# First batch of a conv and MLP-mixer kernel: convolution halo in four row quarters, and another order of its loads, decodes and stores

## The chip, the core and the metric

The kernel runs on one core of a Trainium2 chip. Its engines are TensorE (PE, with a weight load PEld beside the matmuls), VectorE (DVE), ScalarE (ACT), GpSimd (POOL) and SyncE (SP), each with a queue of its own that runs in order, and 16 DMA engines. The metric is the device time of one launch in microseconds, lower is better.

## The reference

```python
# x (8, 4096, 192) float32, weight (8, 7); w_tok1 (4096, 256), w_tok2 (256, 4096),
# w_ch1 (192, 1536), w_ch2 (1536, 192) are float64
w = softmax(weight, axis=-1)                     # 8 heads of 24 channels, 7 taps
x_pad = concat([zeros(B, 6, D), x], axis=1)
xc[b, s, h, g] = sum_k w[h, k] * x_pad[b, s + k, h, g]          # causal convolution
h = maximum(xc.T @ w_tok1, 0) @ w_tok2           # token mixing, for each channel
u = xc + h.T
out = u + maximum(u @ w_ch1, 0) @ w_ch2          # channel mixing, for each token
```

## The kernel before

The eight batches go in groups: the first batch alone, then pairs. The 4096 tokens of a batch are 32 blocks of 128; block `j` holds tokens `128 j` to `128 j + 127` on the partitions. Large products run on TensorE as three products of a high and a low part (`hi*hi + hi*lo + lo*hi`). The four weights come from HBM in 64-bit form, are loaded as pairs of 32-bit words (`dec_raw`, `early_raw`) and put together on chip: one ACT step (Abs, L196) and four VectorE steps (L198, L199, L202, L205), and, where high and low parts are needed, a cast on ACT (L211) and a difference on VectorE (L212). They are all decoded once, during the first batch. Four buffers hold raw words; a load into one waits until the decode before it in that buffer has ended.

`stage1_first` runs the first batch up to token mixing:

- The convolution runs on TensorE. `make_band` builds, from the softmax of the taps `cw`, a `band` matrix per head (128x128, the taps within a block) and a `corner` matrix per head (the 6 tokens that come from the block before). It multiplies and reduces on VectorE (L493, L497), moves the pieces to their place with small matmuls (`moved`, L488) and copies them out on ACT (L504, L507). `keep_busy(n)` issues n transposes of the identity whose results nobody reads.
- The blocks go in four chunks of eight. `x0_load(c)` loads a chunk; chunks 1 to 3 bring the last block of the chunk before once more (9 blocks). `conv_mm(m)` does four heads of a chunk: for each a band matmul on its blocks (L522) and a corner matmul on the blocks one earlier (L523), both over 128 rows. `conv_out(m)` copies the sums to `xc_0`, `xc_1`, `xc_2` and, for the fourth chunk, `u` (L532).
- Eight jobs decode w_tok1, four blocks each, to `t_0` to `t_7`; one decodes half of w_tok2 to `t2s`; three decode thirds of w_ch1 to `w_hi`, `w_lo`. `work` and `behind` say between which decodes the matmuls of convolution and token mixing (`mix`, L453) and the copies stand. `begin(n)` issues a job's ACT step, `woven` its VectorE steps, interleaved with another job's, `next_load()` the next load on SP. After the last job come three loads for w_ch2 (`w2f`) and one for the other half of w_tok2.
- `xc_store(c)` writes the convolved chunks to HBM (`xcd`, on SP), `t1_store(i)` the decoded w_tok1 (`t1d`, on POOL); both are read again by later groups.

The hooks after it are the first batch's second half: `first_mix` (`mix2`: the product with `t2s`, added to `u`), `first_transposed` (the identity matmuls and casts to `own_hi`, `own_lo`), and `first_channel1` for six pairs `p` (L1080, relu to `h_first` on ACT, L1092). `load_u` and `load_next` copy the first four convolved blocks on POOL (L1058) for the first and the second group of tokens. `after()` gives up the pool `p0`, in whose place later tiles such as `h_first` are laid; an instruction that writes there first waits for all users of what lay there.

In later groups the convolution runs on ACT and VectorE (L658, L660) from loads `raw` (L648). A planner, `bg`, sets their place among the matmuls from estimated costs; `bg.lands(9e3)` tells it that a load takes 9 us.

Everything is put on the queues in the order of this code; no scheduler moves instructions.

Of the kernel before, what the change touches and what calls it, by code (L numbers as in the profile page):

```python
# [8 lines left out]
F32 = mybir.dt.float32  # L9
# [130 lines left out]
def conv_mixer_kernel(ctx: ExitStack, tc: tile.TileContext, x, weight, w_tok1, w_tok2, w_ch1, w_ch2, out):  # L140
    nc = tc.nc
    B, S, D = x.shape
    H, K = weight.shape
    G = D // H
# [246 lines left out]

    def stage1_first(pe, p0, pd, late, load_u, load_next, after, thirds, hooks):
        b = GROUPS[0][0]
# [3 lines left out]
        dec = Decoder(pd, 1024, 4, 3)  # L397
        BC = P // 4
        BR = BC + HALO
# [26 lines left out]
        homes = [(pe if c else p0).tile([P, NC + 1, D], F32, name=f"x0_{c}") for c in range(len(chunks))]  # L426
        xcs += [p0.tile([P, NC, D], F32, name=f"xc0_{c}") for c in range(len(chunks) - 1)]
        tops = [p0.tile([P, TJ * JT], F32, name=f"t1_{i}") for i in range(NJ // TJ)]

        def x0_load(c):  # L430
            x0 = homes[c]
            x0s.append(x0)
            j0 = chunks[c].start
            if c == 0:
                nc.gpsimd.memset(x0[:, 0, :], 0.0)
                nc.sync.dma_start(out=x0[:, 1:], in_=xt[:, 0:NC])
            else:
                nc.sync.dma_start(out=x0, in_=xt[:, j0 - 1:j0 + NC])

# [43 lines left out]
        def make_band():  # L483
# [16 lines left out]
            for hs in halves:  # L500
                ps = ps_x.tile([P, P // BC, H2, BC], F32, name="ps_x")
                for b0 in range(P // BC):
                    moved(ps[:, b0], b0 * BC - HALO, hs)
                nc.scalar.copy(out=band[:, hs].rearrange("p h (b c) -> p b h c", c=BC), in_=ps)  # L504
                ps = ps_x.tile([P, H2, BC], F32, name="ps_x")
                moved(ps, P - HALO, hs)
                nc.scalar.copy(out=corner[:, hs, 0:BC], in_=ps)  # L507
                if hs.start == 0:
                    keep_busy(9)

        def conv_mm(m):
            c, part = m // 2, m % 2
            x0 = x0s[c]
            n = NC
            for h2 in range(part * H // 4, (part + 1) * H // 4):
                ps = ps_x.tile([P, TT], F32, name="ps_x")
                convs.setdefault(m, []).append((h2, ps))
                for i in range(2):
                    h = 2 * h2 + i
                    o = ps[:, i * n * G:(i + 1) * n * G].rearrange("p (j g) -> p j g", g=G)  # L520
                    hs = slice(h * G, (h + 1) * G)
                    nc.tensor.matmul(out=o, lhsT=band[:, h], rhs=x0[:, 1:, hs], start=True, stop=False)  # L522
                    nc.tensor.matmul(out=o, lhsT=corner[:, h], rhs=x0[:, :n, hs], start=False, stop=True)  # L523

# [36 lines left out]
        next_load()  # L561
        begin(0)
        make_band()
# [8 lines left out]
        for n in range(nj - 1):  # L572
            if n + 2 < nj:
                begin(n + 1)
            if n == 1:
                conv_mm(2)
            for m in behind.get(n, ()):
                conv_out(m)
            chains = [chains_a[n - 1][2:] if n else [], chains_a[n][:2]]

            if n in (len(quads) - 1, len(quads)):
                woven(chains.pop(0))
            woven(*chains, split(n - 2) if n > 1 and "top" not in jobs[n - 2] else [])
            if n + 2 == nj:
                begin(n + 1)
            for fn in work.get(n, ()):
                fn()
            if n not in (0, 6, 9):
# [6 lines left out]
            if n == 7:  # L595
                load_u(xcs[0])
            if n == 9:
                late()
        n = nj - 1
        mix1_done(0, accs)  # L600
        woven(split(n - 2))
        hooks[0]()
        hooks[1]()
        woven(chains_a[n - 1][2:], chains_a[n][:2])
        next_load()
        woven(split(n - 1))
        load_next(xcs[0])
        for i in range(len(quads)):
            t1_store(i)
        after()  # L610
        hooks[2]()
        woven(chains_a[n][2:])
        next_load()
        woven(split(n))
        for jb, st in zip(later, sts[nj:]):
# [9 lines left out]
    def stage1(gi, pools):  # L625
# [276 lines left out]

    def mix2(gi, q, t2, u, at_once=False, turned=None):
        nb = len(GROUPS[gi])
# [8 lines left out]
        for j in range(TJ):  # L913
# [152 lines left out]

    def first_mix():
        mix2(0, 0, *first["u"], at_once=True)

# [115 lines left out]
    def first_done():  # L1185
# [218 lines left out]
```

## Time and profile before

| | |
|---|---|
| median of 3 runs | 2025.3 us (2024.91 to 2025.76) |
| profiled execution | 2024.59 us |
| its span on the core | 2022.8 us |
| mean granted TensorE clock | 0.998 |
| busy: PE, PEld, DVE, ACT, POOL | 2006.7, 1862.9, 1505.6, 777.0, 218.5 us |
| bytes moved | 260.93 MB, 129 GB/s over the span |

The span is the time from the first to the last record on the core; the execution's own time is 1.8 us more. Busy shares are averages over the whole span, while the change lies in its first 120 us; so the windows and the timelines of that stretch are what to read. In a timeline a row gives start and duration in us, engine, line, operation, and what ended the idle time before it. "SPq" is an issue of a DMA on SP, and its duration holds the time in which SP waited to issue it.

### The profile page before, as it was taken

Reading aid. Unit: us, or ns where it says so; the run is one execution under the profiler, and the core shown is the slowest. Engines: PE = TensorE matmul, PEld = TensorE weight load, DVE = VectorE, ACT = ScalarE, POOL = GpSimd, SP = SyncE. Lnnn points to the kernel's source line nnn. Section 1 sums busy time; section 2 is a strip of 40 time slices with the busy share of each in tenths; the row PEclk is TensorE's granted clock in tenths of the full one; section 3 lists DMA queues with packets and bytes.
Section 4 is the critical chain, followed back from the end, with each engine's and each line's share of the span. In section 5 each row is a group of like instructions: output and inputs, shape, how many; then the busy total and the mean of one; then the engine's idle time right before and its main releaser. Section 6 shows DMA issues by size and latency. Waiting matters only on the chain.

```text
span 2022.8 us, 44729 instructions
## 1 busy us (share of the span) xinstructions
PE 2006.7 (99%) x18667; PEld 1862.9 (92%) x18667; DVE 1505.6 (74%) x3008; ACT 777.0 (38%) x1280; POOL 218.5 (11%) x380
## 2 busy tenths in 40 slices
PE   9999999999999999999999999999999999999999
PEld 9889999999999999998999999999999999999998
DVE  7799998998759998856975689556666666666664
ACT  4676554544333434323333334232233222333322
POOL 0100000001211011110111100111111010011110
PEclk9999999999999999999999999999999999999999
DMA  9855446455455567424664335433233232333310
GB/s 308 282 160 169 132 156 207 155 163 186 132 154 143 155 189 203 125 67 123 170 162 116 106 93 150 146 95 80 53 77 79 74 84 67 79 84 85 85 48 17
DMA packets 280089, 260.93 MB, mean 129 GB/s; under 512 B 188624, under 2 KB 227280, under 8 KB 279888
## 3 DMA queue, kind: packets, MB, share of 16 engines
q1 hardware_dynamic: 257360, 179.80, 31.5%
q0 software_dynamic: 22528, 78.27, 12.9%
q8 instruction: 148, 2.42, 0.5%
q14 instruction: 53, 0.43, 0.1%
HBM read 146.60 MB, written 71.30 MB: 108 GB/s over the span
## 4 chain that ended last, share of the span: by engine, by line
PE 91%; DVE 4%; DMA 2%; SPq 1%; ACT 1%; issue 0%; POOL 0%; ACTq 0%; DVEq 0%
PE ps_x L1080 36%; PE ps_x L1139 23%; PE ps_x L1156 12%; PE ps_x L1157 5%; PE ps_x L959 2%; DVE xc L660 2%; PE ps_a L767 2%; PE ps_a L768 2%; PE ps_a L769 2%; DMA dec_raw<-in_moe_w_tok_dram 1%; DVE hl L1122 1%; PE ps_a L453 1%; PE ps_x L927 1%; PE ps_x L924 1%; PE ps_x L929 1%; PE ps_x L928 1%
## 5 line engine op out<-in xcount | busy, mean ns | idle before, releaser
L1121 ACT ACTIVATE hh<-ps_x 128x512 fp32r<-128x512 f32 x756 | 410.9, 596 | 838.3 <-PE ps_x L1080 838.1
L1122 DVE SCALAR_TENSOR_TENSOR hl<-ps_x,hh 128x512 fp32r<-128x512 f32 x756 | 484.6, 685 | 190.9 <-ACT hh L1121 189.7
L1139 PE MATMUL ps_x<-w,hh 64*128 64x384 f32 x3360 | 483.2, 356 | 2.7 <-ACT hh L1121 2.7
L1139 PE MATMUL ps_x<-w,hl 64*128 64x192 f32 x3360 | 422.0, 248 | 0.4 <-DVE hl L1122 0.4
L660 DVE SCALAR_TENSOR_TENSOR xc<-raw,cw,xc 128x384 f32<-128x384 f32 (+1 forms) x768 | 388.1, 560 | 11.1 <-ACT xc L658 11.1
L1156 PE MATMUL ps_x<-w,hh 128*128 128x384 f32 x1344 | 387.6, 360 | 0.0
L1157 PE MATMUL ps_x<-w,hl 128*128 128x192 f32 x1344 | 336.5, 250 | 0.0
L1080 PE MATMUL ps_x<-other,w_hi 64*128 64x512 f32 x1296 | 336.3, 388 | 0.0
L1080 PE MATMUL ps_x<-own_hi,w_hi 64*128 64x512 f32 x1440 | 331.9, 392 | 1.6 <-ACT own_hi L989 0.6
L1080 PE MATMUL ps_x<-own_lo,w_hi 64*128 64x512 f32 x1440 | 325.9, 388 | 0.0
L1080 PE MATMUL ps_x<-own_hi,w_lo 64*128 64x512 f32 x1440 | 325.8, 388 | 0.0
L1139 PEld LDWEIGHTS ps_x<-w,hl 64*128 64x128 f32 x3360 | 322.2, 188 | 1.8 <-DVE hl L1122 0.9
L1139 PEld LDWEIGHTS ps_x<-w,hh 64*128 64x128 f32 x3360 | 316.2, 185 | 3.9 <-ACT hh L1121 2.9
L1157 PEld LDWEIGHTS ps_x<-w,hl 128*128 128x128 f32 x1344 | 256.6, 191 | 0.0
L1080 PEld LDWEIGHTS ps_x<-other,w_hi 64*128 64x128 f32 x1296 | 235.9, 184 | 22.3
L1156 PEld LDWEIGHTS ps_x<-w,hh 128*128 128x128 f32 x1344 | 252.4, 188 | 0.4 <-DVE hl L1122 0.4
L1080 PEld LDWEIGHTS ps_x<-own_hi,w_hi 64*128 64x128 f32 x1440 | 212.9, 185 | 31.0 <-issue 4.4
L1080 PEld LDWEIGHTS ps_x<-own_hi,w_lo 64*128 64x128 f32 x1440 | 217.8, 185 | 25.1
L1080 PEld LDWEIGHTS ps_x<-own_lo,w_hi 64*128 64x128 f32 x1440 | 218.0, 185 | 24.8
L1080 PE MATMUL ps_x<-other,w_lo 64*128 64x512 f32 x648 | 181.4, 386 | 0.0
L1147 DVE TENSOR_TENSOR osb<-ps_x,osb 128x192 f32<-128x192 f32 x420 | 150.2, 358 | 25.4 <-PE ps_x L959 0.5
L1145 DVE TENSOR_TENSOR osb<-ps_x,u 128x192 f32<-128x192 f32 x140 | 49.8, 356 | 134.9 <-PE ps_x L1139 134.9
(164 smaller groups left out, 2423.6 us busy)
## 6 DMA issues: line engine op xcount, KB each, us to landing
raw<-in_x_dram SPq DMA_DIRECT2D x56, 672.0 KB, 7.2
t<-t2d SPq DMA_DIRECT2D x64, 512.0 KB, 5.7
u<-xcd SPq DMA_DIRECT2D x62, 384.0 KB, 7.3
xcd<-xc POOLq DMA_DIRECT2D x28, 768.0 KB, 8.0
t<-t1p SPq DMA_DIRECT2D x32, 512.0 KB, 4.4
out_dram<-osb POOLq DMA_DIRECT2D x36, 384.0 KB, 3.5
out_dram<-osb SPq DMA_DIRECT2D x27, 384.0 KB, 3.1
t2d<-stage SPq DMA_DIRECT2D x16, 512.0 KB, 4.8
```

What stands on the lines that cost most here:

```text
L660: nc.vector.scalar_tensor_tensor(out=dst, in0=src, scalar=cw[:, h, k:k + 1], in1=dst, op0=ALU.mult, op1=ALU.add)
L767: nc.tensor.matmul(out=ps, lhsT=wh, rhs=xh, start=a, stop=False)
L768: nc.tensor.matmul(out=ps, lhsT=wh, rhs=xl, start=False, stop=False)
L769: nc.tensor.matmul(out=ps, lhsT=wl, rhs=xh, start=False, stop=z)
L1080: nc.tensor.matmul(out=ps, lhsT=w1[w][rows, t[h][2][c], p * P:(p + 1) * P], rhs=t[h][v][rows, c], start=n == 0, stop=n == len(prods) - 1,)
L1121: nc.scalar.activation(out=h["hh", f], in_=ps, func=AF.Relu)
L1122: nc.vector.scalar_tensor_tensor(out=h["hl", f], in0=ps, scalar=0.0, in1=f32(h["hh", f]), op0=ALU.max, op1=ALU.subtract)
L1139: nc.tensor.matmul(out=ps[:, :m], lhsT=h[part, f][ks, ts], rhs=w2[ks, f, :m], start=n == 0 and part == "hh", stop=z and part == "hl",)
L1145: nc.vector.tensor_tensor(out=rows(osb[:, j]), in0=rows(pss[0][:, :D]), in1=tokens(u, i)[:, j], op=ALU.add)
L1147: nc.vector.tensor_tensor(out=osb[:, j], in0=v, in1=osb[:, j], op=ALU.add)
L1156: nc.tensor.matmul(out=ps[:, :2 * D], lhsT=h["hh", f][:, ts], rhs=w2[:, f, :], start=n == 0, stop=False)
L1157: nc.tensor.matmul(out=ps[:, :D], lhsT=h["hl", f][:, ts], rhs=w2[:, f, :D], start=False, stop=z)
```

## The change

1. Halo: `corner` becomes `[P, 4, 2, P]`. Each pair of heads uses 6 rows at partition 0, 32, 64 or 96, so that the corner matmuls take 6 rows and lie in four row quarters, one after the other in the queue. Their other operand is a new tile `halo`, filled by four loads of 6 partitions x 31 blocks x 48 channels on ACT's queue. The chunks are then loaded with 8 blocks each.
2. Band: pieces of 16 columns instead of 32 (`BC = P // 8`), so that VectorE's operations become 22x448 instead of 38x896 and there are twice the small matmuls; `keep_busy` 34 and 4 instead of 54 and 9; the first job's ACT step stands behind the first band copies.
3. Loads: the first weight load is ahead of the first x load. The job of w_tok2 comes ahead of the last of w_tok1.
4. Stores: `xc_store` stood ahead of the second w_ch2 load; now chunks 3 and 0 follow the third w_ch2 load, chunks 1 and 2 the w_tok2 load after it. `t1_store` stays behind `load_next`.
5. `mix2` takes VectorE steps of the first w_ch1 third between its adds; the two other thirds begin later.
6. `t_0` to `t_7`, `xc_1`, `xc_2` lie in a new pool `p1`, given up after `stage1_first`; `xc_0` stays in `p0`.
7. `bg.lands` is told 12 us instead of 9 for the first load of each group of pairs.

```diff
-        BC = P // 4
+        BC = P // 8
...
-        corner = p0.tile([P, H, P], F32, name="corner")
+        corner = p0.tile([P, NQ, 2, P], F32, name="corner")
         nc.gpsimd.memset(corner, 0.0)
+        halo = p0.tile([P, NJ, 2 * G], F32, name="halo")
+        nc.gpsimd.memset(halo[:, 0], 0.0)
+        for g in range(NQ):
+            nc.scalar.dma_start(
+                out=halo[g * QB:g * QB + HALO, 1:], in_=xt[P - HALO:, :NJ - 1, 2 * g * G:2 * (g + 1) * G]
+            )
...
-                nc.sync.dma_start(out=x0, in_=xt[:, j0 - 1:j0 + NC])
+            nc.sync.dma_start(out=x0, in_=xt[:, chunks[c].start:chunks[c].stop])
...
-        jobs = [t1_job(i) for i in range(len(quads))] + [t2_job(0, 0, TT)] + [w1_job(ps) for ps in thirds]
+        nt = len(quads) - 1
+        jobs = [t1_job(i) for i in range(nt)] + [t2_job(0, 0, TT), t1_job(nt)] + [w1_job(ps) for ps in thirds]
...
-                moved(ps, P - HALO, hs)
-                nc.scalar.copy(out=corner[:, hs, 0:BC], in_=ps)
+                for n, g in enumerate(gs):
+                    moved(ps[:, n], g * QB, slice(2 * g, 2 * (g + 1)))
+                nc.scalar.copy(out=corner[:, gs.start:gs.stop, :, 0:BC], in_=ps)
                 if hs.start == 0:
-                    keep_busy(9)
+                    begin(0)
+                    keep_busy(4)
...
-                    nc.tensor.matmul(out=o, lhsT=band[:, h], rhs=x0[:, 1:, hs], start=True, stop=False)
-                    nc.tensor.matmul(out=o, lhsT=corner[:, h], rhs=x0[:, :n, hs], start=False, stop=True)
+                    nc.tensor.matmul(out=sums(ps, i), lhsT=band[:, h], rhs=x0[:, :, hs], start=i == 0, stop=False)
+            if part:
+                for i in range(2):
+                    for g, ps in convs[m - 1] + convs[m]:
+                        rs = slice(g * QB, g * QB + HALO)
+                        nc.tensor.matmul(
+                            out=sums(ps, i), lhsT=corner[rs, g, i],
+                            rhs=halo[rs, chunks[c].start:chunks[c].stop, i * G:(i + 1) * G], start=False, stop=i == 1,
+                        )
...
+        next_load()
         x0_load(0)
-        next_load()
-
-        keep_busy(54)
+        keep_busy(34)
...
-            6: [lambda: mix(4), lambda: mix(5)], 8: [lambda: mix(6, 7)],
+            6: [lambda: mix(4), lambda: mix(5)], 7: [lambda: mix(6)],
...
-            if n == 8:
-                for c in (3, 0, 1, 2):
-                    xc_store(c)
...
+        load_u(xcs[0])
+        woven(chains_a[nt][2:])
+        woven(split(nt))
+        woven(chains_a[nt + 1])
+        mix(nt)
...
         mix1_done(0, accs)
-        woven(split(n - 2))
-        hooks[0]()
+        hooks[0](chains_a[nt + 2][2:])
...
-        woven(split(n - 1))
+        woven(split(nt + 3))
+        for c in (3, 0):
+            xc_store(c)
         load_next(xcs[0])
-        for i in range(len(quads)):
-            t1_store(i)
         after()
         hooks[2]()
-        woven(chains_a[n][2:])
+        woven(chains_a[nt + 4][2:])
         next_load()
-        woven(split(n))
+        woven(split(nt + 4))
+        for c in (1, 2):
+            xc_store(c)
+        for i in range(len(quads)):
+            t1_store(i)
...
-                    done["load", q2, part] = bg.lands(9e3)
+                    done["load", q2, part] = bg.lands(9e3 if q2 else 12e3)
```

VectorE's queue at the end of the w_tok1 decodes, before. `t_7` is the last block of w_tok1; the first `dec_top` of 128x1024 is the half of w_tok2, those of 128x768 are thirds of w_ch1:

```order
L205 SCALAR_TENSOR_TENSOR t_6_131<-dec_raw,t_6_131 128x1024
L198 TENSOR_SCALAR t_7_132<-t_7_132 128x1024
L199 TENSOR_SCALAR t_7_132<-t_7_132 128x1024
L202 SCALAR_TENSOR_TENSOR t_7_132<-dec_raw,t_7_132 128x1024
L205 SCALAR_TENSOR_TENSOR t_7_132<-dec_raw,t_7_132 128x1024
L198 TENSOR_SCALAR dec_top<-dec_top 128x1024
L199 TENSOR_SCALAR dec_top<-dec_top 128x1024
L202 SCALAR_TENSOR_TENSOR dec_top<-early_raw,dec_top 128x1024
L198 TENSOR_SCALAR dec_top<-dec_top 128x768
L205 SCALAR_TENSOR_TENSOR dec_top<-early_raw,dec_top 128x1024
```

The same place after the change:

```order
L205 SCALAR_TENSOR_TENSOR t_6_140<-dec_raw,t_6_140 128x1024
L198 TENSOR_SCALAR dec_top<-dec_top 128x1024
L199 TENSOR_SCALAR dec_top<-dec_top 128x1024
L202 SCALAR_TENSOR_TENSOR dec_top<-dec_raw,dec_top 128x1024
L205 SCALAR_TENSOR_TENSOR dec_top<-dec_raw,dec_top 128x1024
L212 TENSOR_TENSOR t2s<-dec_top,t2s 128x2x512
L198 TENSOR_SCALAR t_7_141<-t_7_141 128x1024
L199 TENSOR_SCALAR t_7_141<-t_7_141 128x1024
L202 SCALAR_TENSOR_TENSOR t_7_141<-early_raw,t_7_141 128x1024
L205 SCALAR_TENSOR_TENSOR t_7_141<-early_raw,t_7_141 128x1024
```

The five steps of the w_tok2 half, its low part (L212) with them, moved ahead of the last block of w_tok1.

SP's queue around the stores of the convolution, before. `x2` stands for two in a row; `in_moe_w_ch_dram` of 128x4x384 is w_ch2, `in_moe_w_tok_dram` of 128x2x1024 the other half of w_tok2, `raw` the next batches' x:

```order
L538 DMA xcd_75<-xc_1_123 128x1536
L538 DMA xcd_75<-xc_2_124 128x1536
L232 DMA dec_raw<-in_moe_w_ch_dram 128x4x384 x2
L232 DMA dec_raw<-in_moe_w_tok_dram 128x2x1024
L648 DMA raw_759<-in_x_dram 128x14x96
```

After:

```order
L553 DMA xcd_75<-xc_0_131 128x1536
L232 DMA dec_raw<-in_moe_w_tok_dram 128x2x1024
L553 DMA xcd_75<-xc_1_132 128x1536
L553 DMA xcd_75<-xc_2_133 128x1536
L670 DMA raw_753<-in_x_dram 128x14x96
```

The stores moved behind the w_ch2 loads (two of them ahead of, two behind the w_tok2 load); ahead of the first row shown stands now `xcd<-u` and ahead of that the last w_ch2 load.

ACT's queue at the first channel mixing, after, where the waits of an instruction stand in brackets (DMAHW4 is the landing of a load or store that SP issued, here of `xcd<-xc_0`; Pool is the second copy of `xc_0`):

```order
L211 CAST w_hi<-dec_top 128x3x256 [waits DVE_49]
L1116 ACTIVATE h_first<-ps_x 128x512 [waits DMAHW4_49,PE_49,Pool_49]
L1116 ACTIVATE h_first<-ps_x 128x512 [waits PE_49]
L211 CAST w_hi<-dec_top 128x3x256 [waits DVE_49]
L196 ACTIVATE w2f<-dec_raw 128x768 [waits DMAHW0_49]
```

Before the change these rows are the same but for line and semaphore numbers; what moved is the place of the store and of the copy that the second row waits for.

More of the change, by code (lines that the diff above doesn't have):

```diff
@@ L388, in mix1_accs, with stage1_first @@
         return [ps_a.tile([P, TT], F32, name=f"ps_a{kc}") for kc in range(KC)]
-    def stage1_first(pe, p0, pd, late, load_u, load_next, after, thirds, hooks):
+    def stage1_first(pe, p0, p1, pd, late, load_u, load_next, after, thirds, hooks):
         b = GROUPS[0][0]
@@ L422, in stage1_first @@
         band = p0.tile([P, H, P], F32, name="band")
[L423 removed]
+        corner = p0.tile([P, NQ, 2, P], F32, name="corner")
         nc.gpsimd.memset(corner, 0.0)
[L426 to L428 removed]
+        halo = p0.tile([P, NJ, 2 * G], F32, name="halo")
[4 more added lines that the diff above has]
+            )
+        homes = [(pe if c else p0).tile([P, NC, D], F32, name=f"x0_{c}") for c in range(len(chunks))]
+        xcs += [(p1 if c else p0).tile([P, NC, D], F32, name=f"xc0_{c}") for c in range(len(chunks) - 1)]
+        tops = [p1.tile([P, TJ * JT], F32, name=f"t1_{i}") for i in range(NJ // TJ)]
         def x0_load(c):
@@ L504, in make_band @@
                 nc.scalar.copy(out=band[:, hs].rearrange("p h (b c) -> p b h c", c=BC), in_=ps)
-                ps = ps_x.tile([P, H2, BC], F32, name="ps_x")
-                moved(ps, P - HALO, hs)
-                nc.scalar.copy(out=corner[:, hs, 0:BC], in_=ps)
+                ps = ps_x.tile([P, 2, 2, BC], F32, name="ps_x")
+                gs = range(hs.start // 2, hs.stop // 2)
+                for n, g in enumerate(gs):
+                    moved(ps[:, n], g * QB, slice(2 * g, 2 * (g + 1)))
+                nc.scalar.copy(out=corner[:, gs.start:gs.stop, :, 0:BC], in_=ps)
                 if hs.start == 0:
-                    keep_busy(9)
+                    begin(0)
+                    keep_busy(4)
         def conv_mm(m):
@@ L514, in conv_mm, with sums @@
             n = NC
+            def sums(ps, i):
+                return ps[:, i * n * G:(i + 1) * n * G].rearrange("p (j g) -> p j g", g=G)
             for h2 in range(part * H // 4, (part + 1) * H // 4):
@@ L561, in stage1_first @@
         next_load()
-        begin(0)
         make_band()
@@ L569, in stage1_first @@
             4: [lambda: mix(2), lambda: mix(3)], 5: [lambda: conv_mm(6), lambda: conv_mm(7)],
-            6: [lambda: mix(4), lambda: mix(5)], 8: [lambda: mix(6, 7)],
+            6: [lambda: mix(4), lambda: mix(5)], 7: [lambda: mix(6)],
         }
-        for n in range(nj - 1):
-            if n + 2 < nj:
+        for n in range(nt + 1):
+            if n < nt:
                 begin(n + 1)
@@ L578, in stage1_first @@
                 conv_out(m)
+            if n == nt:
+                begin(n + 1)
             chains = [chains_a[n - 1][2:] if n else [], chains_a[n][:2]]
-            if n in (len(quads) - 1, len(quads)):
+            if n == nt:
                 woven(chains.pop(0))
-            woven(*chains, split(n - 2) if n > 1 and "top" not in jobs[n - 2] else [])
-            if n + 2 == nj:
-                begin(n + 1)
+            woven(*chains)
             for fn in work.get(n, ()):
                 fn()
-            if n not in (0, 6, 9):
+            if n not in (0, 6):
                 next_load()
@@ L901, in conv_mixer_kernel, with mix2 @@
     NQ = P // QB
-    def mix2(gi, q, t2, u, at_once=False, turned=None):
+    def mix2(gi, q, t2, u, at_once=False, turned=None, between=()):
         nb = len(GROUPS[gi])
@@ L932, in mix2 @@
                 two, one = flat(u)[:, j, 0], flat(u)[:, j, 1]
+                if between:
+                    between.pop(0)()
                 if not at_once:
@@ L1065, in first_next, with first_mix @@
         first["next"] = first_load(xc, TJ)
-    def first_mix():
-        mix2(0, 0, *first["u"], at_once=True)
+    def first_mix(between):
+        mix2(0, 0, *first["u"], at_once=True, between=between)
     def first_transposed():
@@ L1172, in conv_mixer_kernel @@
     hp = None
-    pe_ctx, p0_ctx, pd_ctx, ht_ctx = (ExitStack() for _ in range(4))
+    pe_ctx, p0_ctx, p1_ctx, pd_ctx, ht_ctx = (ExitStack() for _ in range(5))
     pe = pe_ctx.enter_context(tc.tile_pool(name="pe", bufs=1))
     pd = pd_ctx.enter_context(tc.tile_pool(name="pd", bufs=1, side="right"))
+    p1 = p1_ctx.enter_context(tc.tile_pool(name="p1", bufs=1, side="right"))
     p0 = p0_ctx.enter_context(tc.tile_pool(name="p0", bufs=1, side="right"))
```

31 lines of the change are left out of this document (15 added, 16 removed).

## The prediction

> **What bounds the kernel now.** I read the page's busy times and chain first, then its first 140 us by windows, then the timelines of the engines there.
>
> ```profile
> PE 2006.7 (99%) x18667; PEld 1862.9 (92%) x18667; DVE 1505.6 (74%) x3008; ACT 777.0 (38%) x1280; POOL 218.5 (11%) x380
> PE 91%; DVE 4%; DMA 2%; SPq 1%; ACT 1%; issue 0%; POOL 0%; ACTq 0%; DVEq 0%
> ```
>
> PE is busy 2006.7 of 2022.8 us, and 91% of the chain is PE's. What the first batch loses at its end stays lost: nothing behind it has slack worth a microsecond. Everything that the change touches, but for one number in the planner, lies in the first 120 us. By windows (span; then busy us and instructions of PE, PEld, DVE, ACT, POOL; PE clock, DMA share, GB/s):
>
> ```profile
> 25.00:30.40 5.40, 5.40 (x33) 5.40 (x34) 5.13 (x7) 2.06 (x4) 0.77 (x1) 1.00 1.05 383
> 61.10:66.40 5.30, 4.51 (x20) 2.96 (x21) 4.46 (x7) 4.63 (x7) 5.04 (x6) 0.73 1.02 356
> 77.00:82.00 5.00, 4.15 (x23) 3.37 (x22) 3.44 (x5) 4.01 (x6) 0.00 (x0) 1.00 0.65 196
> 82.00:87.60 5.60, 5.04 (x30) 4.49 (x28) 4.38 (x5) 2.00 (x2) 0.57 (x1) 1.00 0.31 73
> 100.00:120.00 20.00, 17.21 (x139) 16.30 (x140) 18.73 (x41) 10.55 (x19) 0.75 (x1) 1.00 0.38 119
> 120.00:140.00 20.00, 20.00 (x156) 18.55 (x157) 17.75 (x42) 17.06 (x24) 0.75 (x1) 1.00 0.60 194
> ```
>
> From 25 to 30 us PE, DVE (5.13 of 5.40) and the DMA engines (1.05) are all full: three resources share the early stretch. From 120 us PE is full and the others are not. Whether a saving on PE before 57 us counts is thus decided by VectorE, which decodes the weights. Its timeline (start, duration; in brackets idle before and releaser):
>
> ```profile
> 6.79 1.08 DVE L493 TENSOR_TENSOR u<-u,cw 38x896 f32<-38x896 f32 x1
> 21.38 0.69 DVE L198 TENSOR_SCALAR t<-t 128x1024 f32<-128x1024 f32 x1 [2.82 <-ACT t L196]
> 40.48 1.23 DVE L205 SCALAR_TENSOR_TENSOR t<-dec_raw,t 128x1024 uint32<-128x1024 uint32 x1
> 44.33 1.23 DVE L205 SCALAR_TENSOR_TENSOR t<-dec_raw,t 128x1024 uint32<-128x1024 uint32 x1
> 52.09 0.96 DVE L202 SCALAR_TENSOR_TENSOR dec_top<-dec_raw,dec_top 128x768 uint32<-128x768 uint32 x1
> 56.12 0.35 DVE L383 SCALAR_TENSOR_TENSOR h<-ps_a,h 128x192 fp32r<-128x192 f32 x1
> 63.67 0.94 DVE L205 SCALAR_TENSOR_TENSOR dec_top<-dec_raw,dec_top 128x768 uint32<-128x768 uint32 x1
> 64.54 0.55 DVE L199 TENSOR_SCALAR dec_top<-dec_top 128x768 uint32<-128x768 uint32 x1
> 69.62 0.96 DVE L212 TENSOR_TENSOR w_lo<-dec_top,w_hi 128x768 fp32r<-128x768 f32 x1 [0.90 <-ACT w_hi L211]
> 77.94 0.56 DVE L198 TENSOR_SCALAR w2f<-w2f 128x768 f32<-128x768 f32 x1 [1.26 <-ACT w2f L196]
> 86.64 1.23 DVE L212 TENSOR_TENSOR t2s<-dec_top,t2s 128x1024 fp32r<-128x1024 f32 x1 [1.11 <-ACT t2s L211]
> 97.90 0.77 DVE L660 SCALAR_TENSOR_TENSOR xc<-raw,cw,xc 128x192 f32<-128x192 f32 x2 [1.46 <-ACT xc L658]
> 115.17 0.68 DVE L212 TENSOR_TENSOR t2s<-dec_top,t2s 128x512 fp32r<-128x512 f32 x1
> ```
>
> The reader is to see that from 21.38, when the third block of w_tok1 lands, to the end of the last of these blocks at 44.33 + 1.23 = 45.56 the decodes run one behind the other, 3.85 us each (45.56 less 41.71). At 86.64 and 115.17 stand the two results that PE itself waits for:
>
> ```profile
> 9.39 1.38 PE L488 MATMUL ps_x<-u,turn 38*128 38x128 f32 x10
> 40.64 0.49 PE L522 MATMUL ps_x<-x,band 128*128 128x192 f32 x2
> 45.84 5.36 PE L453 MATMUL ps_a<-xc,t 128*128 128x192 f32 x32
> 87.92 0.35 PE L925 MATMUL ps_x<-h,t2s 128*128 128x192 f32 x1 [0.82 <-DVE t2s L212]
> 115.91 0.36 PE L925 MATMUL ps_x<-h,t2s 128*128 128x192 f32 x1 [2.79 <-DVE t2s L212]
> ```
>
> Those two waits are where a shift of VectorE becomes time. On ACT, SP and POOL:
>
> ```profile
> 66.67 1.09 ACT L1092 ACTIVATE h_first<-ps_x 128x512 f32<-128x512 f32 x2 [0.81 <-issue]
> 68.75 0.83 ACT L211 CAST w_hi<-dec_top 128x768 fp32r<-128x768 f32 x1 [0.99 <-DVE dec_top L205]
> 97.43 0.78 ACT L658 ACTIVATE xc<-raw,cw 128x192 f32<-128x192 f32 x2
> 48.02 0.35 SPq L538 DMA_DIRECT2D xcd<-u  x1
> 55.80 9.26 SPq L232 DMA_DIRECT2D dec_raw<-in_moe_w_ch_dram  x2
> 79.05 6.92 SPq L648 DMA_DIRECT2D raw<-in_x_dram  x2
> 58.38 0.83 POOL L1058 COPY u<-xc 128x768 f32<-128x768 f32 x1 [32.61 <-PE ps_x L922]
> 59.16 6.98 POOL L445 DMA_DIRECT2D t1d<-t  x8
> xcd<-u SPq DMA_DIRECT2D x1, 768.0 KB, 10.2
> xcd<-xc SPq DMA_DIRECT2D x3, 768.0 KB, 13.0
> xcd<-xc POOLq DMA_DIRECT2D x28, 768.0 KB, 8.0
> out_dram<-osb SPq DMA_DIRECT2D x27, 384.0 KB, 3.1
> t1d<-t POOLq DMA_DIRECT2D x8, 512.0 KB, 10.0
> q1 hardware_dynamic: 257360, 179.80, 31.5%
> ```
>
> **The change, part by part.**
>
> *Convolution.* A chunk of eight blocks takes 45.84 - 40.64 = 5.20 us, half of it band and half corner matmuls. Four side by side make the second half 0.65 at best, 2.60 at worst: 0 to 1.95 us a chunk, 0 to 7.8 in all, ahead of the first product with t2s at 56.1. What hides it is VectorE's decode of the last w_tok1 block (next but one), so I count 0.
>
> *Band.* Four VectorE operations on 38x896 (1.08 each) become four on 22x448, near 0.6: 2 us less ahead of 11 us. VectorE then waits for a load anyway (2.82 at 21.38): 0. PE moves 10 pieces a half where it moved 5 (1.38 us): between 0 and 1.4 us more a half, beside the fillers that are cut from 54 and 9 to 34 and 4: 0.
>
> *Halo loads.* 4 x 186 runs of 192 B, 143 KB, in the full stretch, less 96 KB that each later x load saves, one of which lies ahead of the third block. All its bytes at 383 GB/s are 0.4 us; by the hardware queue's mean packet (31.5% of 16 x 2022.8 us over 257360, 0.040 us) 744 x 0.040 / 16 = 1.9. I take 0.4, since the packets are small, and keep +1.9 and -0.3 (no cost, and the 96 KB at 383 GB/s) as ends. The Trainium skill's page "DMA: Bandwidth & Descriptors" (section on why a DMA increments its semaphore by 16) says that the number of engines for a transfer divides its slowest dimension; a tile of 6 partitions would then run on 6 of 16. No run here shows it yet; by it 744 x 0.040 / 6 would be 5.0, and the sum below 4.6 higher. The fourth halo load also waits for the landing of the first, with the softmax's exp queued behind it on ACT; the 2 us saved on the band cover it.
>
> *Order of decodes.* After the block that ends at 40.48 + 1.23 = 41.71 now come the half of w_tok2 (3.85, the same shape), its rounding on ACT (1.11 idle in the row at 86.64), the low part (1.23), and only then the last w_tok1 block (3.85): 41.71 + 3.85 + 1.11 + 1.23 + 3.85 = 51.75, with the halo 52.2. Half of a 5.36 us mix follows, where before a whole one stood: the first L383 comes near 54.8 instead of 56.12, a gain of 1.3. Between it and the end of the second w_ch1 third's L205 were 64.61 - 56.12 = 8.5 us. Added there are L202 and L205 of the first third (0.96 and 0.94), L198 and L199 of the second (0.55 each) and some 0.5 for its ACT step: 12.0. So that L205 ends at 66.8, where it ended at 64.61.
>
> *The stores of the convolution.* This is the part that decides. At 48.02 SP issued them, ahead of the two w_ch2 loads that take until 65. Now `xcd<-u` and `xcd<-xc_0` stand behind the last w_ch2 load, which waits for the L205 just worked out to give its buffer back. With three issues at 0.35 the second store is out at 67.9. The first relu of channel mixing (before at 66.67) writes h_first where xc_0 lay, and so waits for that store to land and for POOL's second copy of xc_0; that copy waits for `xcd<-u` to land. Landing: 3.1 us is the floor (half the size, a quiet stretch), 13.0 the ceiling (the same stores in the full stretch). I take 8.0, the 28 stores of the same size in later stretches, as the one load ahead has the same 768 KB. The relu then starts near 76.2 (POOL's 0.83 falls beside the 0.4 between the stores). Behind it on ACT stand the last third's w_hi cast, for which VectorE's w_lo waits, and all of w_ch2: relu pair 1.09 and cast 0.83 put the w_lo at 78.1, against 69.62. PE runs out of ps_x buffers meanwhile and idles, at a lower clock afterwards, as at 61 to 66 (0.73); VectorE stays the bound. From that w_lo to t2s's end were 86.64 + 1.23 - 69.62 = 18.25 us, of them 1.26 waiting for the last w_ch2 load, which is there by then: 17.0. The t2s ends at 95.1 instead of 87.87: **+7.2**.
>
> *The stores of w_tok1.* POOL's eight issues stand behind its copy: they begin at 76.2, not 59.16. 6.98 and 10.0 later, at 93.2, the last has landed; before, the same sum gives 76.1 and SP was released at 79.05, so 93.2 to 96.2. SP's load of the next batch's x waits for it, with five t loads and two w_tok2 loads behind. From the second x load at 79.05 + 6.92 = 85.97 to ACT's L658 (97.43) were 11.5 us; from 95.5 that gives 107.0, **+9.6** where the t2s chain begins that PE waits for at 115.91. The two delays overlap. Whether all of 9.6 reaches PE depends on the chain's slack, of which 1.46 is seen at 97.90. I take halfway between 7.2 and 9.6: 8.4.
>
> *mix2's interleaving, the pools, 12e3 for 9e3.* The first is in the 12.0 above; the pools make the waits told; the number shifts first pair rows behind 120 us, where VectorE has 2.25 of 20 us idle: 0, ends -1 and +1.5.
>
> Sum: the profiled execution took 2024.6 (span 2022.8 and 1.8 around it); 2024.6 + 8.4 = 2033.0. The median of the runs, 2025.3, is 0.7 above that execution; rounded I say 2033.5 for it.
>
> **Rivals.** *Faster.* The early stretch is really DMA's: 3 MB of stores leave it, 8.2 us at 383 GB/s, and the w_ch1 and w_ch2 loads come that much sooner. The place is VectorE between 45.56 and 66; it decides if the second third's L205 ends before 59, so that the stores (8.0) have landed by 67. Then the quarters' saving counts as well, t2s comes 4 us sooner, and the time is about 2020.5. For it speak the DMA share of 1.05 and the 2.82 of idle at 21.38; against it, that the decodes between stand end to end and that the last of them now carries 6.2 us more ahead of it. *No change.* The DMA engines are near idle by the time of the stores (0.65 and 0.31 in the windows from 77 us), so that they land at the floor: relu at 71.2, w_lo 73.1, t2s at 90.1, +2.2, of which PE's gain ahead of it and 0.82 of wait return part, while the second delay shrinks with the first: 2024 to 2028, about 2025.5. Against it: the load issued just ahead shares the engines with both stores, 2.3 MB, 6 us at 383 GB/s. *The quarters run one after the other*, or lose what they gain to switching: the convolution takes its 5.2 a chunk as before, VectorE covers it, and the time is the forecast's. *The halo loads spread over few engines*, six, say: 744 packets of 0.040 us are then 5.0 on each instead of 0.4 in all, the third block's decode begins up to 4.6 later and all that follows it with it: 2038. Nothing in this trace loads six partitions, so that it speaks neither way.
>
> **Chances.** The forecast, with or without quarters side by side, 0.63, of its own between 2028 and 2039.5 (landing 3.1 to 13.0 is -4.9 to +5.0, halo up to +1.5); late halo loads, 0.05; no change, 0.17; faster, 0.15. A difference under 0.2% (4 us) can't be told from none here. The range is 2023.0 to 2039.5: it leaves out most of the faster case and little above. Faster 0.15, same 0.17, slower 0.68.
>
> **What would show it.** SP's rows: `xcd<-u` issued near 67 and not 48, the t1d stores near 76, the next x load past 92. ACT's first h_first row with an idle of 6 us or more ahead, named after a DMA or POOL. VectorE idle ahead of the w_lo near 78, t2s near 95, PE's second such wait near 124 and after that windows full as before. The convolution's chunk below 5.2 shows the quarters, the third block's decode near 21.8 the halo's price. It is wrong if the first relu starts before 71, if the last w_tok1 decode ends well before 50, or if PE makes the time up behind 120 us.

## The result and the profile after

The changed kernel takes 2032.55 us (median of 6 runs, 2029.95 to 2034.73) against 2025.11 (6 runs, 2021.07 to 2025.76). The ratio is 1.0041, 95% interval 1.0030 to 1.0051: slower by 7.4 us, where 2033.5 was forecast. The profiled execution is the slowest of the six, 2034.73, with a span of 2033.0; so its distance to the profile before is 10.2 in the span, not 7.4.

Its page has the same work and a longer span:

```profile
PE 2008.3 (99%) x18662; PEld 1862.3 (92%) x18662; DVE 1504.0 (74%) x3008; ACT 777.3 (38%) x1280; POOL 216.3 (11%) x380
PE 92%; DMA 3%; DVE 3%; ACT 1%; SPq 1%; issue 0%; POOL 0%; DVEq 0%; ACTq 0%
```

No engine is busier by more than 1.6 us, and in the chain DMA grows from 2% to 3%: a wait was added. The windows of the start (span; busy us and instructions of PE, PEld, DVE, ACT, POOL; PE clock, DMA share, GB/s) show where:

```profile
61.10:66.40 5.30, 4.30 (x26) 2.66 (x28) 3.23 (x6) 4.87 (x7) 0.00 (x0) 1.00 0.37 135
66.40:77.00 10.60, 4.04 (x32) 2.40 (x28) 4.41 (x6) 0.83 (x1) 2.21 (x3) 0.97 0.78 266
82.00:87.60 5.60, 5.60 (x41) 4.63 (x40) 5.39 (x9) 4.09 (x8) 0.00 (x0) 0.89 1.02 387
120.00:140.00 20.00, 16.64 (x101) 15.71 (x98) 16.81 (x38) 9.03 (x14) 0.00 (x0) 0.83 0.35 106
```

From 66.4 to 77 us the engines mostly stand: PE is busy for 4.0, VectorE for 4.4 and ACT for 0.8 of 10.6 us. The DMA engines are little used from 61 to 66 us (0.37) and full from 82 to 87 (1.02), where before they were full first (1.02) and little used then (0.31): the stores are issued 20 us later (68.05 against 48.02). From 120 us, where PE was full, it now loses 3.4. Timelines of ACT, SP and POOL (start, duration, operation; idle before and what ended it):

```profile
77.04 1.08 ACT L1116 ACTIVATE h_first<-ps_x 128x512 f32<-128x512 f32 x2 [8.62 <-DMA xcd<-xc]
107.99 0.79 ACT L680 ACTIVATE xc<-raw,cw 128x192 f32<-128x192 f32 x2
68.05 0.50 SPq L553 DMA_DIRECT2D xcd<-u  x1
68.59 0.43 SPq L553 DMA_DIRECT2D xcd<-xc  x1
94.74 1.26 SPq L670 DMA_DIRECT2D raw<-in_x_dram  x2
74.79 0.83 POOL L1082 COPY u<-xc 128x768 f32<-128x768 f32 x1 [47.91 <-DMA xcd<-u]
75.56 6.13 POOL L446 DMA_DIRECT2D t1d<-t  x8
```

The first relu stands 8.62 us and is released by the store of `xc_0`, which was issued at 68.59. On VectorE and PE:

```profile
22.51 0.69 DVE L198 TENSOR_SCALAR t<-t 128x1024 f32<-128x1024 f32 x1 [2.40 <-ACT t L196]
48.36 1.23 DVE L212 TENSOR_TENSOR t2s<-dec_top,t2s 128x1024 fp32r<-128x1024 f32 x1 [1.95 <-ACT t2s L211]
52.21 1.22 DVE L205 SCALAR_TENSOR_TENSOR t<-early_raw,t 128x1024 uint32<-128x1024 uint32 x1
66.60 0.95 DVE L205 SCALAR_TENSOR_TENSOR dec_top<-dec_raw,dec_top 128x768 uint32<-128x768 uint32 x1
78.88 0.96 DVE L212 TENSOR_TENSOR w_lo<-dec_top,w_hi 128x768 fp32r<-128x768 f32 x1 [7.61 <-ACT w_hi L211]
94.39 1.22 DVE L212 TENSOR_TENSOR t2s<-dec_top,t2s 128x1024 fp32r<-128x1024 f32 x1 [1.11 <-ACT t2s L211]
124.87 0.68 DVE L212 TENSOR_TENSOR t2s<-dec_top,t2s 128x512 fp32r<-128x512 f32 x1
40.22 2.76 PE L530 MATMUL ps_x<-x,band 128*128 128x192 f32 x16
42.91 0.93 PE L535 MATMUL ps_x<-halo,corner 6*128 6x192 f32 x16
43.77 5.47 PE L454 MATMUL ps_a<-xc,t 128*128 128x192 f32 x32
53.49 2.87 PE L454 MATMUL ps_a<-u,t 128*128 128x192 f32 x16 [1.65 <-DVE t L205]
56.06 0.39 PE L942 MATMUL ps_x<-h,t2s 128*128 128x192 f32 x1
77.69 2.13 PE L1104 MATMUL ps_x<-own_hi,w_hi 64*128 64x512 f32 x6 [6.56 <-ACT h_first L1116]
95.67 0.36 PE L947 MATMUL ps_x<-h,t2s 128*128 128x192 f32 x1 [0.54 <-DVE t2s L212]
125.61 0.53 PE L947 MATMUL ps_x<-h,t2s 128*128 128x192 f32 x1 [3.35 <-DVE t2s L212]
```

The last chunk of the convolution takes 43.77 - 40.22 = 3.55 us instead of 5.20, and its 16 corner matmuls 0.86 of them: the quarters do run side by side. Fewer rows alone don't give that: before the change ten matmuls of 38 rows by 128 columns took 1.38 us, and nine of 128 rows by 128 columns 1.20. But the first product with t2s comes at 56.06, as at 56.12 before: VectorE's `t_7` ends at 53.4, and PE, which waits 1.65 us for it, still has half a mix to do. So the saving of 1.65 a chunk went into PE's waits, and part of it, as the run with the convolution alone shows below, into a lower clock. PE's two t2s waits end 7.75 and 9.70 us later than before (95.67 against 87.92, 125.61 against 115.91): the second delay adds 1.95 to the first.

### The profile page after: what moved, and what is told of

It reads as the page before. It is cut to its first block, busy times and chain, and to the rows that moved or that the text cites. A ratio compares the mean times of both kernels' runs of the same rounds, so it can differ in the third digit from the quotient of the medians.

```text
span 2033.0 us, 44726 instructions
## 1 busy us (share of the span) xinstructions
PE 2008.3 (99%) x18662; PEld 1862.3 (92%) x18662; DVE 1504.0 (74%) x3008; ACT 777.3 (38%) x1280; POOL 216.3 (11%) x380
## 4 chain that ended last, share of the span: by engine, by line
PE 92%; DMA 3%; DVE 3%; ACT 1%; SPq 1%; issue 0%; POOL 0%; DVEq 0%; ACTq 0%
PE ps_x L1104 37%; PE ps_x L1163 23%; PE ps_x L1180 13%; PE ps_x L1181 6%; PE ps_x L983 2%; PE ps_a L789 2%; PE ps_a L790 2%; PE ps_a L791 2%; DMA dec_raw<-in_moe_w_tok_dram 2%; DVE xc L682 1%; PE ps_x L946 1%; PE ps_x L949 1%; PE ps_x L951 1%; PE ps_x L950 1%; PE ps_a L785 1%; DMA early_raw<-in_moe_w_tok_dram 1%
## 5 line engine op out<-in xcount | busy, mean ns | idle before, releaser
L1104 PE MATMUL ps_x<-own_hi,w_hi 64*128 64x512 f32 x1440 | 336.8, 396 | 9.4 <-ACT h_first L1116 6.6
L1163 PEld LDWEIGHTS ps_x<-w,hl 64*128 64x128 f32 x3360 | 327.1, 188 | 0.9
L1163 PEld LDWEIGHTS ps_x<-w,hh 64*128 64x128 f32 x3360 | 321.8, 184 | 0.9
```

Of the source, the lines that this page charges most:

```text
L1104: nc.tensor.matmul(out=ps, lhsT=w1[w][rows, t[h][2][c], p * P:(p + 1) * P], rhs=t[h][v][rows, c], start=n == 0, stop=n == len(prods) - 1,)
L1163: nc.tensor.matmul(out=ps[:, :m], lhsT=h[part, f][ks, ts], rhs=w2[ks, f, :m], start=n == 0 and part == "hh", stop=z and part == "hl",)
```

## The experiments

Two theories were to be told apart: that the late stores cost the time, through the relu's wait and through POOL's queue; or that the new order of decodes and the halo loads do, and the stores fill a gap. A third question came up on the way: what the planner's number does.

**Stores early again, all else as changed.**

```diff
+        for c in (3, 0, 1, 2):
+            xc_store(c)
         next_load()
         late()
...
-        for c in (3, 0):
-            xc_store(c)
...
-        for c in (1, 2):
-            xc_store(c)
```

> The changed kernel with all four stores of the convolution back ahead of the w_ch2 loads; all else as changed. Theory (the first relu waits for the landing of the late store, everything behind it shifts): the first h_first row starts near 68 without an idle named after a DMA, w_lo of the last third near 71, t2s ends near 88.5, PE's second t2s wait ends near 116 to 117, and the time comes back to 2025 to 2027 (up to 1.1 above the kernel before, by the later third block). Rival (the new order of decodes or the halo loads cost the time, the stores only fill a gap): at least 2030.

Measured: 2022.65 us (11 runs), ratio to the kernel before 0.9990 (0.9981 to 0.9999): 9.9 below the changed kernel, and a little below the kernel before, further than expected. Its ACT and PE:

```profile
67.02 1.08 ACT L1114 ACTIVATE h_first<-ps_x 128x512 f32<-128x512 f32 x2
54.37 0.39 PE L940 MATMUL ps_x<-h,t2s 128*128 128x192 f32 x1
87.59 0.35 PE L945 MATMUL ps_x<-h,t2s 128*128 128x192 f32 x1 [0.55 <-DVE t2s L212]
115.57 0.36 PE L945 MATMUL ps_x<-h,t2s 128*128 128x192 f32 x1 [2.79 <-DVE t2s L212]
```

The relu starts without a wait, and both t2s waits are back where they were (87.92 and 115.91). The place of the stores is shown to be the cost. The gain behind that is not from this stretch; the planner's experiments below find it.

**The stores late, alone, in the kernel before.**

```diff
-            if n == 8:
-                for c in (3, 0, 1, 2):
-                    xc_store(c)
...
         woven(split(n - 1))
+        for c in (3, 0, 1, 2):
+            xc_store(c)
         load_next(xcs[0])
```

> The kernel before with nothing changed but the four stores, which go behind the last w_ch2 load. Theory: issued near 65, landing 8 to 13 later, so the first relu starts at 74 to 79 instead of 66.7, t2s ends 8 to 11 later than 87.9, and the time is 2032 to 2036. Rival (the loss needs the new decode order, the old one has slack for the stores): 2024 to 2027.

Measured: 2031.86 us, ratio 1.0032 (1.0021 to 1.0044), +6.8.

```profile
63.97 0.50 SPq L538 DMA_DIRECT2D xcd<-u  x1
72.65 1.09 ACT L1091 ACTIVATE h_first<-ps_x 128x512 f32<-128x512 f32 x2 [7.91 <-DMA xcd<-xc]
90.97 0.35 PE L924 MATMUL ps_x<-h,t2s 128*128 128x192 f32 x1 [0.55 <-DVE t2s L212]
121.65 0.53 PE L924 MATMUL ps_x<-h,t2s 128*128 128x192 f32 x1 [3.36 <-DVE t2s L212]
```

The same wait, with the same releaser, in the old order of decodes. The relu came somewhat sooner than I expected (8.2 after the first store was out at 64.47, in spite of three stores behind it), and the time is just below the range. The end of t2s was missed: PE's first t2s wait ends 3.05 later than before (90.97 against 87.92), not 8 to 11; the second ends 5.74 later, so nearly half of it comes by the second delay. In the changed kernel both are larger, since the new order of decodes lets the stores go 4.1 later still (68.05 against 63.97): PE's second wait ends 4.0 later there. This profile is of the fastest of the six executions, and 1.8 of its loss is given back between 920 and 1010 us, at a stall that the planner's experiments below are about.

**The stores of w_tok1 ahead of POOL's copy, in the changed kernel.**

```diff
+        for i in (nt, *range(nt)):
+            t1_store(i)
         load_next(xcs[0])
...
-        for i in range(len(quads)):
-            t1_store(i)
```

> The changed kernel with the eight stores of w_tok1 ahead of POOL's second copy (the last block first, so that none starts before the decodes are done near 53). Theory of two overlapping delays: the relu still starts near 77 and t2s ends near 95.6, but the next x load no longer waits for the w_tok1 stores; it waits for the decode of the second w_tok2 half (ends near 93.3), ACT's first convolution step of the next pair comes near 105.5 instead of 108.0, PE's second t2s wait ends near 123 instead of 125.6, and the time is about 2.5 below the changed kernel, 2030. Rival (only the relu's delay counts, the rest has slack): as the changed kernel, 2032 to 2033.

Measured: 2030.50 us, ratio 1.0026 (1.0015 to 1.0038): 2.05 below the changed kernel, with intervals that overlap.

```profile
55.33 6.27 POOL L446 DMA_DIRECT2D t1d<-t  x8 [28.44 <-DVE t L205]
79.77 1.08 ACT L1116 ACTIVATE h_first<-ps_x 128x512 f32<-128x512 f32 x2 [9.75 <-DMA xcd<-xc]
98.36 0.36 PE L947 MATMUL ps_x<-h,t2s 128*128 128x192 f32 x1 [0.54 <-DVE t2s L212]
107.86 0.79 ACT L680 ACTIVATE xc<-raw,cw 128x192 f32<-128x192 f32 x2
126.39 0.53 PE L947 MATMUL ps_x<-h,t2s 128*128 128x192 f32 x1 [2.83 <-DVE t2s L212]
```

The relu itself was later here (79.77), since this execution, the slowest of its seven, runs 1.6 to 2.7 us behind from 48 us on, where VectorE waits 3.55 us for the first half of t2s and not 1.95; so the absolute times that I expected were not met (PE's second wait ends at 126.39, not near 123). The distances were. From PE's first t2s wait to the next pair's first convolution step are 107.86 - 98.36 = 9.5 us, against 107.99 - 95.67 = 12.3 in the changed kernel; and from PE's first t2s wait to its second 126.39 - 98.36 = 28.0, as in the kernel before (115.91 - 87.92 = 28.0), against 125.61 - 95.67 = 29.9 in the changed kernel. So in the profiles the second delay is worth 1.9 us of PE's 9.7, and the relu's the other 7.75. The times alone don't show it, as their intervals overlap.

**The convolution's part alone, in the kernel before.** Its edit is the convolution's part of the diff above: `BC = P // 8`, `corner`, `halo`, the x loads of 8 blocks, `make_band` (with `keep_busy(9)` left) and `conv_mm`.

> The kernel before with the convolution's part alone: halo loads, row quarters, band of 16 columns; order of loads, decodes and stores and the fillers as before. Theory (VectorE's decodes hide it): a chunk takes 3.5 instead of 5.2 on PE, the first product with t2s still comes near 56, the third block's decode 0.5 to 1.1 later, the time 2025 to 2026.5. Rival (PE bounds the stretch from 25 to 56 us): the first product with t2s near 51, the time 2019 to 2021.

Measured: 2026.44 us, ratio 1.0005 (0.9996 to 1.0014): no difference that can be told, and the rival's 2019 to 2021 did not come.

```profile
17.66 4.66 PE L528 MATMUL ps_x<-x,band 128*128 128x192 f32 x16
34.77 0.93 PE L533 MATMUL ps_x<-halo,corner 6*128 6x192 f32 x16
55.22 0.35 PE L933 MATMUL ps_x<-h,t2s 128*128 128x192 f32 x1
```

The quarters are there, and the first product with t2s comes 0.9 earlier than before and not 5 or 6. But it was not VectorE that held PE here: the last mix starts at 49.79, when `t_7` has been done since 46.46, and PE is busy for 46.5 of the 46.6 us from 9.4 to 56. What took the saving is mostly PE's clock. Windows from 10 to 22 us, of the kernel before and of this one:

```profile
10.00:22.00 12.00, 11.44 (x75) 10.74 (x75) 8.07 (x11) 5.39 (x9) 0.00 (x0) 1.00 1.07 361
10.00:22.00 12.00, 12.00 (x57) 11.56 (x55) 5.54 (x7) 4.70 (x7) 0.00 (x0) 0.57 1.06 349
```

At 0.57 some 5.2 us of full clock are missing, of the 6.6 that four chunks save; the first chunk's 16 band matmuls take 4.66 instead of the 2.76 of later chunks. The doubled number of small matmuls adds about 1 us a half (2.41 against 1.38 for the first). All seven profiles of kernels with the new band have 0.57 to 0.86 there, the four without it 1.00. What lowers the clock isn't shown: the fall begins between 10 and 13 us in all seven, ahead of the first corner matmul, and this kernel has its fillers as before. So the run shows that the convolution's part gains nothing as it stands, and not what the quarters would give at full clock. That VectorE would hide that as well is argued only: it is busy for 25.04 of the 25.60 us from 30.4 to 56, and in the kernel with early stores a first product with t2s that comes 1.75 earlier than before (54.37) moves PE's next t2s wait by 0.33.

**The planner's number alone**, in the kernel before, and taken back in the kernel with early stores:

```diff
-                    done["load", q2, part] = bg.lands(9e3)
+                    done["load", q2, part] = bg.lands(9e3 if q2 else 12e3)
```

> The kernel before with only the planner's number changed, 12e3 for 9e3 at the first load of each group of pairs. Theory (the number, and nothing in the first batch, removed PE's stall near 930 us, where ACT waits 4.8 us for a late x load): ACT's wait there falls to near 2.4, PE's wait of 2.7 on hh is gone, and the time falls 2 to 3.3, to 2021.8 to 2023. Rival (that stall moved only because the changed kernels come there at another phase): 2024.5 to 2025.5.

> The changed kernel with its stores ahead of the w_ch2 loads and the planner's number back at 9e3. Theory (all that this kernel gained was the planner's): 2024.5 to 2026.5, with PE's wait near 930 us back. Rival (quarters and new decode order bring the gain): 2022 to 2023.3.

Measured: 2020.87 us for the number alone, ratio 0.9982 (0.9973 to 0.9990), -3.8; 2026.01 with the number taken back, ratio 1.0005 (0.9996 to 1.0014). ACT and PE of the kernel before, then ACT of the kernel with the number alone:

```profile
933.15 1.12 ACT L658 ACTIVATE xc<-raw,cw 128x384 f32<-128x384 f32 x2 [4.78 <-POOL raw L650]
934.17 1.06 ACT L1121 ACTIVATE hh<-ps_x 128x512 fp32r<-128x512 f32 x2
934.80 0.44 PE L1139 MATMUL ps_x<-w,hh 64*128 64x384 f32 x2 [2.70 <-ACT hh L1121]
```

```profile
932.40 2.14 ACT L658 ACTIVATE xc<-raw,cw 128x384 f32<-128x384 f32 x4 [2.30 <-POOL raw L650]
```

Before, ACT reaches a convolution row at 928.4, stands 4.78 us because the x load's tile is not ready, and the relu `hh` behind it on ACT, for which PE waits, is late by that much: PE loses 2.70. With 12e3 the row stands later in ACT's queue, ACT waits 2.30, and PE's wait is gone. The windows of 900 to 1000 us, before and with the number:

```profile
900.00:1000.00 100.00, 96.89 (x876) 90.90 (x876) 75.77 (x150) 34.53 (x58) 15.55 (x27) 0.98 0.58 152
900.00:1000.00 100.00, 99.47 (x929) 90.88 (x930) 78.45 (x156) 34.77 (x58) 15.51 (x27) 1.00 0.57 152
```

So all that the early-store kernel gained is this number's. The changed kernel holds a gain at the same stall: against the kernel before, VectorE's `hl` rows (one behind each relu `hh`) are 13.0 us late ahead of it, at the row that starts at 920 us before, and 9.9 behind it, from 1100 us on, 3.1 less. The number alone gives 3.6 between these rows, and the late stores alone, without the number, 1.8. No run takes the number out of the changed kernel, so how much of its 3.1 is the number's and how much comes from reaching the stall later is open.

**PE's wait near 115 us filled.** In the kernel with early stores, and in the kernel before with the planner's number:

```diff
                 elif nb == 1:
                     nc.tensor.matmul(out=ps[:, :2 * D], lhsT=wh, rhs=h1[:, kc, :, :n], start=a, stop=False)
+                    if gi == 0 and q == 2 and j == 0 and z:
+                        fill = ps_x.tile([P, TT], F32, name="ps_x")
+                        for k in range(22):
+                            nc.tensor.transpose(out=fill[:, k % TJ * P:(k % TJ + 1) * P], in_=ident, identity=ident)
```

> The changed kernel with early stores, and 22 transposes of the identity (about 2.4 us, results unread) in PE's queue inside the wait of 2.8 us near 115. Theory (a wait of this length is followed by some 3 to 5 us at half clock in some executions, worth 1.6 each time): the granted clock stays 1.00 from 115 to 120 us and the median falls by 0.8 to 1.6 below the same kernel without them, to 2021 to 2022. Rival (VectorE bounds what follows, or the dip does not depend on PE's own work): 2022.4 to 2023.

> The kernel before with the planner's 12e3 and the 22 transposes. Theory (quarters and decode order are worth nothing once the stores are early): within 1 us of the changed kernel with early stores and the same fillers. Rival (they are worth the 1.7 us by which the first product with t2s came earlier): 1 to 2 us above it.

Measured: 2020.29 us (ratio 0.9977, 0.9968 to 0.9986) and 2020.00 us (0.9975, 0.9966 to 0.9984). Windows from 115 to 120 us of the kernel before, of the kernel with early stores, and of the same with the fillers:

```profile
115.00:120.00 5.00, 4.09 (x28) 4.10 (x29) 4.83 (x13) 0.67 (x1) 0.00 (x0) 1.00 0.01 3
115.00:120.00 5.00, 4.43 (x20) 4.43 (x21) 4.40 (x12) 0.69 (x1) 0.00 (x0) 0.66 0.01 3
115.00:120.00 5.00, 4.58 (x39) 3.98 (x35) 4.33 (x10) 3.09 (x5) 0.00 (x0) 1.00 0.35 108
```

After a wait of 2.8 us the granted clock falls to 0.66 in one execution and stays at 1.00 in another; with the wait filled it stayed at 1.00 in all three profiles taken. (The third row is of the slowest of that kernel's eleven executions, in which the wait ends at 119.23; from 120 to 125 us it has 1.00 too.) Of the other eight, six show the dip, the changed kernel among them. One of the three is the kernel before, which shows no dip unfilled either, so two of them speak for the fillers. Between the first and the 25th of VectorE's `hl` rows (103 and 165 us before) the executions without the dip lose 0.0 to 0.1 us against the kernel before, those with it 0.7 to 2.9, four of the six 1.6 to 1.7. The median fell by more than expected with early stores (2.4) and by 0.9 in the kernel before, whose two profiles (the second is that with the planner's number) show no dip there; why its phase is kinder is open. Both kernels beat the kernel before and the changed one, and are within 0.3 us of each other: the rewritten convolution (with its lower clock) and the decode order are worth nothing that can be measured here.

**Halo loads behind the third block.**

```diff
-        for g in range(NQ):
-            nc.scalar.dma_start(
-                out=halo[g * QB:g * QB + HALO, 1:], in_=xt[P - HALO:, :NJ - 1, 2 * g * G:2 * (g + 1) * G]
-            )
...
         x0_load(1)
         next_load()
+        for g in range(NQ):
+            nc.sync.dma_start(
+                out=halo[g * QB:g * QB + HALO, 1:], in_=xt[P - HALO:, :NJ - 1, 2 * g * G:2 * (g + 1) * G]
+            )
```

> The changed kernel with early stores and the fillers, and the four halo loads moved from ACT's queue at the start to SP's queue behind the load of the third w_tok1 block. Theory (the halo loads delay that block by about 1.3 us, and VectorE's chain behind it carries this to the end of the batch): the third block's decode begins near 21 as in the kernels without halo loads, instead of 21.5 to 23.0, and the median falls by 1.0 to 1.5 below the same kernel with early halo loads, to 2019 to 2019.5. Rival (the block's landing swings by itself, or the chain has slack): 2020 to 2021.

Measured: 2023.89 us, ratio 0.9999 (0.9990 to 1.0008): 3.6 above the same kernel with early halo loads (2020.29), and the two intervals don't meet. The expectation failed. VectorE and SP of that kernel, then SP of the kernel with early stores and halo loads:

```profile
20.62 0.68 DVE L198 TENSOR_SCALAR t<-t 128x1024 f32<-128x1024 f32 x1
31.31 0.69 DVE L198 TENSOR_SCALAR t<-t 128x1024 f32<-128x1024 f32 x1 [1.29 <-ACT t L196]
8.53 5.85 SPq L570 DMA_DIRECT2D halo<-in_x_dram  x4
14.42 2.28 SPq L232 DMA_DIRECT2D dec_raw<-in_moe_w_tok_dram  x1
```

```profile
10.78 1.95 SPq L232 DMA_DIRECT2D dec_raw<-in_moe_w_tok_dram  x1
```

The third block came earlier, as expected, but the four small loads hold SP for 5.85 us, and the next block's load is issued at 14.42 and not at 10.78. The fifth block's decode starts at 31.31, against 29.36 in the early-store kernel without fillers, whose profile is of its median execution, and `t_7` ends 3.0 later than there: more than the third had gained. The DMA share is 1.05 from 25 to 32 us, so the stretch is short of DMA, and a moved load moves the wait.

## Why the prediction was right, by its steps

- *The relu's wait*, the step that decided: second store out at 67.9 forecast, issued at 68.59; relu at 76.2 forecast, 77.04; w_lo 78.1, 78.88; t2s's end 95.1, 95.61. The landing of 8.0 was well chosen: 77.04 - 69.02 = 8.0. Shown from both sides, by taking the late stores out (-9.9) and by making the stores late and nothing else (+6.8, PE's two waits ending 3.05 and 5.74 later).
- *The stores of w_tok1*: issued from 76.2 forecast, 75.56; next x load between 93.2 and 96.2, 94.74; ACT's first step of the next pair 107.0, 107.99. I took halfway between the two delays, 8.4; PE's wait ended 9.7 later, so 0.9 of the 10.6 at ACT's step was slack and the rest reached PE: the term was 1.3 too small. Without the wait for these stores PE's distance shrank by 1.9.
- *Quarters hidden by VectorE*: `t_7` ends at 53.4 (52.2 forecast), and PE waits for it; the first product with t2s at 56.06 was to come 1.3 earlier than before and came 0.06 earlier. The convolution alone gives no measurable change, but there the reason is another, the clock of 0.57 from 10 to 22 us.
- *Band*: 0 forecast, with up to 1.4 more a half on PE. VectorE's operations did fall to 0.61 each. PE's first half took 2.38 for 1.38, its second 3.64, above the end that I gave, at the lower clock (0.72 from 10 to 22 us), which the prediction had put at nothing; VectorE's `t_7` covers it in the changed kernel.
- *Halo loads*: 0.4 forecast with 1.9 as the end. In the six profiles with early halo loads the third block's decode starts between 21.5 and 23.0 (mean 22.3), in the four without between 20.2 and 21.4 (mean 21.0): 1.3, nearer to the end than to my value (the order of loads differs as well in all but one of the six, which has 22.6). From 2 to 13 us of the changed kernel's profile the halo's queue has 768 packets that take 9.0% of the 16 engines' time: 15.8 us, 0.021 a packet and not the 0.040 that I took. That is 1.0 if all 16 engines share them and 2.6 on six. By the rule of the Trainium skill's page "DMA: Bandwidth & Descriptors" (section on why a DMA increments its semaphore by 16), that the number of engines divides the slowest dimension, six engines would carry them, and the estimate was 5.0. The trace doesn't name the engines, so the rule stays open here; the price of 5.0 did not come.
- *The planner's number*: I set it to 0 with -1 and +1.5 as ends. This step failed: alone it is -3.8. The wait of 4.78 on ACT and 2.70 on PE stood in the trace of before at 930 us; I looked for the number's effect behind 120 us, where VectorE is full, and not along the whole program at the rows that it moves. So not all of the change acts in the first 120 us, as I had written ahead of the prediction.
- *The clock* after PE's second wait: not in the sum. It cost 1.7 in the profiled execution.

The profiled sum then goes: +9.7 at PE's second wait, +10.6 at the first `hl` row, +12.2 at the 25th with the dip, +13.0 at the row of 920 us (the last 0.8 comes between 430 and 730 us, and its cause is open), and, behind the stall near 930 us, +9.9 at the last; with what these rows leave open, 10.2 in the span. The forecast of +8.4 came near because a missing gain of 3.1 and missing losses of 1.3 (which has the halo's excess in it), 0.9, 1.7 and 0.8 partly cancelled. One of the prediction's signs of being wrong, that PE makes the time up behind 120 us, came in part: 3.1 of 13.0. The mechanism is shown; part of the nearness of 2033.5 to 2032.55 is luck.

Of the rivals, the faster one (DMA bounds the early stretch, and the moved stores help it) is answered by the early-store kernel: the DMA share from 51 to 66 us is 0.41 with the stores late and 1.03 with them early, and nothing comes earlier by it (the second w_ch1 third's L205 starts at 66.60 and 65.29). "No change" needed the stores to land in 3.1 us; they took 8.0.

## What to carry to other kernels

A store isn't free to move back because nobody reads it soon: the tile that it reads from may be the place of the next one, and whoever writes there first waits for it to land. Before moving a transfer, list what is laid where its source lies, and who waits for its queue. And look for the effect of a planner's number where the rows that it moves wait now, over the whole program: here one number was worth 3.8 us, and the rewritten convolution and the new order of decodes nothing that could be measured. And read the granted clock of a stage that was made shorter: the one here ran part of its work at half clock.

## What was new about the hardware

- Four matmuls of 6 rows on four row quarters: 16 of them in 0.86 us (42.91 to 43.77) against 2.60 for the 16 full ones of a chunk before (half of 5.20), 3.0 times. The Trainium skill's page "TensorE: Matmul & The Clock Gate" (Part 3, measured speedup) has 3.07 for four quarters of 32 rows with 512 columns; at 192 columns this agrees.
- A wait of 2.8 us is enough for a clock of 0.66 over the next 5 us, in some executions and not in others at the same place. The same page (Part 1) has a free-running window of about 3.4 us; that the dip comes and goes between executions agrees with that. In four of the six profiles with the dip the wait was 2.79 to 2.83 us, shorter than that window.
- The granted clock can be 0.57 over 12 us in which PE's records leave no gap (12.00 of 12.00 us busy from 10 to 22 us, with the convolution alone); why is open.
- The landing of the third block swings by 1.2 us between profiles of kernels that are alike up to there (20.17 to 21.38), and single executions of one kernel differ by up to 6 us (2022.66 to 2028.70 with early stores and the old number): a difference of 1 us needs medians of many runs here.
